# Three pairs of 1024 tokens instead of two, with the attention visits packed closer ahead of them

## The chip, the cores and the metric

The kernel runs on one core of a Trainium2 chip. The metric is the time on the device, in microseconds (us): the median of three runs of the kernel before is 894.93 us (894.25 to 895.53). A profiled execution of the same kernel took 893.7 us, of which 891.9 us lie between its first and its last instruction (the span).

## The reference, cut to what matters

Sliding-window attention (one half of the heads with a plain window of 32 keys, the other with 32 keys at a stride of 4) makes the tokens of a feed-forward layer:

```python
scores = scale * np.matmul(q, k.transpose(0, 1, 3, 2))      # q, k, v: 8 x 8 heads x 576 x 64
scores = np.where(masks[None], scores, -1e9)
attn = np.exp(scores - scores.max(-1)); attn /= attn.sum(-1) + 1e-9
x = np.matmul(attn, v).transpose(0, 2, 1, 3).reshape(4608, 512)
h = x @ w_in                                                # 512 -> 2048
sp = np.maximum(h, 0.0) + np.log1p(np.exp(-np.abs(h)))      # softplus
out = (h * erf(sp)) @ w_out                                 # 2048 -> 512
```

All is float32. The kernel keeps that accuracy by splitting each matmul operand into a high and a low part ("hi", "lo") and adding three products: hi*hi, hi*lo and lo*hi.

## The kernel before, in words

**Attention.** The work is cut into 72 units of 4 blocks of 64 queries. A visit (`attend`, `turn`, `mask_max`, `exponents`, `normalize`) takes one or two units and does, for units whose turn it is, transposes (L261) and values (L280), and for units three further on, scores (L222). VectorE (DVE) adds the mask and takes the maximum (L233), ScalarE (ACT) does the exponentials (L243) and copies finished rows out of PSUM (L322), GpSimd (POOL) multiplies by the inverse sums (L256). Masks of new units wait until ACT has copied the rows of the old ones out of the same PSUM banks. Finished rows go to HBM (`store_x`) and come back as the tokens of the feed-forward part.

**The feed-forward part** takes 9 chunks of 512 tokens. Per chunk there are 8 steps t (two blocks of 128 hidden features each), and each step has two half steps, numbered x = 2t and 2t+1. Three ways of doing the first product are in use:

- Chunks 0 to 2 (`mm1`, L526): 12 matmuls of 128x512 per half step into one PSUM bank `h`, which DVE copies out (`take`, L672).
- Chunks 3 and 4 (`mm1_fast`, L651): seven block products in place of eight (Winograd's form of Strassen's scheme) over the halves of one chunk, 42 matmuls of 128x256 per step; `take_fast` adds the products up.
- Chunks 5 to 8 as two pairs of 1024 tokens (`mm1_big`, L842): the same seven products with a whole chunk as each half, 42 matmuls of 128x512 per two blocks of features, so one such call serves two steps' worth of tokens. `take_big` adds them up (L850 to L862).

The block sums of the weights ("A11, S1 ...") are made once (`build`, x = 29 to 47) and kept in HBM (`ws`); `load_left` brings them back. The block sums of the tokens (B11, B21, B22, T1 to T4) are made by three kinds of job: `*_less` (DVE subtracts), `*_hi` (ACT writes the high part) and `*_lo` (DVE writes the low part).

**After h:** softplus and erf on ACT (L676, L679; L875, L952 in the pairs; each needs its table loaded), a product on DVE (L684, L879), the split into ghi and glo (L690, L691), and the second product on TensorE (PE), `mm2`, 12 matmuls of 128x512 per block of features into four PSUM banks (L715).

**Order.** All is one hand-written order; each engine works through its own instructions in that order and waits where a semaphore says so. First come 14 visits to single units, then 80 half steps x = 0 to 79 (chunks 0 to 4), then 34 *periods*. A period i does the second product of one item (24 matmuls): items 0 and 1 are the last two steps of the loop, then come A0 to A7 (first chunk of the pair), B0 to B7 (second chunk), A8 to A15, B8 to B15. Only the periods in `BIG` (0 to 7 and 16 to 23) also do a first product `mm1_big(d)`; the others (8 to 15, 24 to 33) have only the 24 matmuls. Items of kind B were put into HBM (`kept_g`) and come back by `load_g`; their ghi is cast by ACT, that of the other items by DVE. A period with a first product runs four groups of products with a quarter of the second product (6 matmuls) behind each:

```python
for u in pending: exponents(u)      # ACT: the units scored in the period before
split_item(item, 1)                 # ghi, glo of the item's second block
third(0); jobs(...); quarter()      # products 0, 1 and their take_big
third(1); ... Erf of A, B of d-1 ...; quarter()
... multiply_big("A", d-1); split_item(ahead, 0); third(2); turn(ready); quarter()
third(3); quarter(); attend(ready, scored); ... mask_max(scored)
```

`visits` says at which half steps (`PACE`) and in which periods (`late`) attention is visited. Before, two units are visited at 21 half steps from 17 to 65 and one unit at 9, 11 and 14; the last nine units are taken in periods 0 to 4. `FORE` and `AFT` say at which half step or period the jobs for a pair's token sums run.

## Time and profile before

| what | before |
|---|---|
| median of the runs | 894.93 us |
| profiled execution | 893.7 us, span 891.9 us |
| TensorE (PE) busy | 874.4 us, 98% |
| weight loads (PEld) | 718.1 us, 81% |
| VectorE (DVE) | 649.0 us, 73% |
| ScalarE (ACT) | 575.3 us, 65% |
| GpSimd (POOL) | 78.2 us, 9% |
| HBM traffic | 132.87 MB read, 41.94 MB written |

A row of a timeline is: start in us from the span's start, length in us, engine, line, operation, output<-inputs, shapes, count, and in brackets the idle time ahead of it with what ended it. Matmuls are pipelined, so the length of one matmul is longer than the distance to the next; what a stream of them costs is read from the starts. A row of the table by stretches is: stretch, its length, then the busy time and the count of instructions of each engine, the granted TensorE clock, the share of time that DMA engines are busy, and GB/s. A row of the groups is: line, engine, operation, names, shapes, count, then busy us and mean ns of one, then idle us before and what ended it.

### The profile page before, as it was taken

How to read it: one execution, taken by the hardware profiler on the slowest of the kernel's cores; microseconds unless marked ns; L12 is line 12 of the kernel's file. 1: busy time of each engine (PE TensorE's matmuls, PEld its weight loads, DVE VectorE, ACT ScalarE, POOL GpSimd, SP SyncE). 2: the span in 40 equal slices, each digit the busy share in tenths (PEclk: the TensorE clock that was granted, in tenths of full speed). 3: DMA queues.
4: the chain of work that ended last, by engine and by line, in shares of the span. 5: the costliest groups of instructions: out<-in, count | busy, mean ns of one | idle time of the engine just before them, and what ended most of it. 6: DMA issues, size and time to landing. Idle time of an engine off the chain costs nothing.

```text
span 891.9 us, 21528 instructions
## 1 busy us (share of the span) xinstructions
PE 874.4 (98%) x8470; PEld 718.1 (81%) x8470; DVE 649.0 (73%) x1623; ACT 575.3 (65%) x1265; POOL 78.2 (9%) x97
## 2 busy tenths in 40 slices
PE   7799999999999999999999999999999999999998
PEld 3367778888888888889889998888888888888886
DVE  5888878986789897767876886777566647575622
ACT  6889888886787786778877644764544434445321
POOL 2212110000111100111110000010000000000000
PEclk9999999999999999999999999999999999999999
DMA  8874444461678778589777753564449125442441
GB/s 284 293 252 150 125 143 133 149 205 55 226 256 299 277 255 295 194 318 311 243 246 262 261 184 137 194 238 170 166 161 358 48 82 208 158 156 81 149 134 49
DMA packets 67015, 176.24 MB, mean 198 GB/s; under 512 B 8288, under 2 KB 14688, under 8 KB 62816
## 3 DMA queue, kind: packets, MB, share of 16 engines
q1 hardware_dynamic: 66624, 174.32, 56.8%
q8 instruction: 67, 1.10, 0.5%
q10 hardware_dynamic: 288, 0.52, 0.2%
q14 instruction: 36, 0.29, 0.1%
HBM read 132.87 MB, written 41.94 MB: 196 GB/s over the span
## 4 chain that ended last, share of the span: by engine, by line
PE 92%; DVE 3%; ACT 2%; DMA 1%; issue 1%; POOL 0%; SPq 0%; POOLq 0%; DVEq 0%
PE acc L715 43%; PE h L526 14%; PE tx L842 9%; PE h L842 9%; PE h L651 5%; PE tx L651 4%; PE sp L280 3%; PE sp L222 3%; PE sp L261 1%; DMA dbl<-in_w_in_dram 1%; PE h L362 1%; ACT prob L243 1%; DVE s L684 0%; DVE w L463 0%; PE acc L280 0%
## 5 line engine op out<-in xcount | busy, mean ns | idle before, releaser
L715 PE MATMUL acc<-wout_hi,ghi 128*128 128x512 f32 x576 | 227.7, 395 | 0.2 <-DVE dbl L729 0.2
L715 PE MATMUL acc<-wout_lo,ghi 128*128 128x512 f32 x576 | 224.8, 390 | 0.0
L715 PE MATMUL acc<-wout_hi,glo 128*128 128x512 f32 x576 | 158.9, 389 | 0.0
L715 PEld LDWEIGHTS acc<-wout_hi,glo 128*128 128x128 f32 x576 | 108.1, 188 | 22.8
L715 PEld LDWEIGHTS acc<-wout_hi,ghi 128*128 128x128 f32 x576 | 108.3, 188 | 21.5 <-DVE dbl L729 0.6
L715 PEld LDWEIGHTS acc<-wout_lo,ghi 128*128 128x128 f32 x576 | 108.3, 188 | 21.0
L256 POOL TENSOR_TENSOR prob<-prob,rinv 128x256 f32<-128x256 f32 x72 | 70.7, 987 | 478.3 <-DVE rinv L255 230.0
L243 ACT ACTIVATE prob<-prob,nmax 128x64 f32<-128x64 f32 x288 | 96.4, 339 | 9.7 <-DVE nmax L233 9.3
L526 PE MATMUL h<-x,win 128*128 128x512 f32 x384 | 96.6, 394 | 0.6 <-DVE hc L672 0.6
L526 PEld LDWEIGHTS h<-x,win 128*128 128x128 f32 x384 | 71.2, 188 | 16.3 <-DVE hc L672 1.0
L233 DVE CUSTOM_DVE_ANT_0 prob<-sp,cst 128x64 f32<-128x64 f32 x288 | 45.2, 219 | 31.3 <-ACT rows L322 19.7
L676 ACT ACTIVATE s<-hc 128x1024 f32<-128x1024 f32 x40 | 42.5, 1062 | 37.1 <-DVE hc L665 22.5
L875 ACT ACT_TABLE_LOAD x16 | 20.5, 1283 | 70.8 <-DVE dbl L850 36.3
L322 ACT COPY rows<-sp 128x128 f32<-128x128 f32 (+7 forms) x167 | 27.8, 307 | 51.2 <-PE sp L222 51.1
L691 DVE TENSOR_TENSOR glo<-s,ghi 128x512 fp32r<-128x512 f32 x78 | 54.3, 696 | 2.7
L672 DVE COPY hc<-h 128x512 f32<-128x512 f32 x48 | 33.0, 688 | 30.1 <-PE h L526 29.8
L243 ACT ACTIVATION_READ_ACCUMULATOR prob<-prob,nmax 128x1 f32 x288 | 54.9, 191 | 0.0
L676 ACT ACT_TABLE_LOAD x40 | 51.3, 1283 | 0.7
L679 ACT ACT_TABLE_LOAD x40 | 51.3, 1283 | 0.7
L684 DVE TENSOR_TENSOR s<-hc,s 128x1024 f32<-128x1024 f32 x39 | 48.9, 1255 | 1.5 <-ACT s L679 1.5
L842 PE MATMUL h<-win 128*128 128x512 f32 x192 | 49.1, 391 | 0.0
L842 PE MATMUL tx<-win 128*128 128x512 f32 x192 | 49.1, 391 | 0.0
(176 smaller groups left out, 1518.2 us busy)
## 6 DMA issues: line engine op xcount, KB each, us to landing
win<-ws SPq DMA_DIRECT2D x32, 1024.0 KB, 5.4
win<-ws SPq DMA_DIRECT2D x32, 768.0 KB, 4.9
v<-in_v_dram SPq DMA_DIRECT2D x72, 256.0 KB, 4.4
qk<-in_qk_dram SPq DMA_DIRECT2D x48, 272.0 KB, 4.3
dbl<-in_w_in_dram SPq DMA_DIRECT2D x16, 512.0 KB, 4.3
dbl<-in_w_out_dram SPq DMA_DIRECT2D x16, 512.0 KB, 3.8
ws<-x SPq DMA_DIRECT2D x32, 256.0 KB, 2.9
qk<-in_qk_dram SPq DMA_DIRECT2D x24, 288.0 KB, 4.5
```

The lines of the kernel that those rows point to most:

```text
L233: nc.vector.tensor_tensor_reduce(out=pr[:, g, :], in0=sps[h][:, u % 2, p, :], in1=mask[QUADS.index(kinds(u, p))], scale=-SCALE, scalar=HUG ...
L243: nc.scalar.activation(out=probs[u][:, j, :], in_=probs[u][:, j, :], func=AF.Exp, scale=-1.0, bias=nmax[:, j:j + 1], accum_out=sums[u][:, ...
L256: nc.gpsimd.tensor_tensor(probs[u], probs[u], rinv.broadcast_to([P, 2 * PARTS, KEYS]), op=ALU.mult)
L526: nc.tensor.matmul(h, win_at[:, ftp, j, cc // 2, w, cc % 2, :], x[cc], start=(k == 0 and i == 0), stop=(k == CC - 1 and i == 2))
L651: nc.tensor.matmul((h, bank)[b][:, half * HN:(half + 1) * HN], w[:, k, wi, c, :], x[:, xi, c, :], start=(c == 0 and n == 0), stop=(c == 1 ...
L672: nc.vector.tensor_copy(out=hs[t][:, j], in_=h)
L676: nc.scalar.activation(out=ls[t], in_=hs[t], func=AF.Softplus)
L679: nc.scalar.activation(out=ls[t], in_=ls[t], func=AF.Erf)
L684: nc.vector.tensor_tensor(out=e, in0=hs[t], in1=ls[t], op=ALU.mult)
L691: nc.vector.tensor_tensor(out=glo, in0=e, in1=ghi.bitcast(F32), op=ALU.subtract)
L715: nc.tensor.matmul(args["out"], args["lhsT"], args["rhs"], start=args["start"], stop=args["stop"])
L842: nc.tensor.matmul(bank_, w[:, wi, c, :], x[c][:, xi, :], start=(c == 0 and n == 0), stop=(c == 1 and n == 2))
```

## The change

Chunks 3 and 4 leave the loop of half steps and become a first pair of 1024 tokens, so the loop ends after x = 47 (was 79), there are 50 periods, and `BIG` holds 0 to 7, 16 to 23 and 32 to 39. `mm1_fast`, `take_fast`, the jobs of `right` and their buffers go. Attention takes two units at 9, 13, 15 and at every odd half step from 17 to 39, none from 40 to 47, and the remaining units two at a time in periods 0 to 7 and 16 to 19. In `mm1` the first half step of a step writes bank `h` and the second writes bank `tx`; from t = 16 on the first one's copy is done by ACT (`late_take`). The token sums of the first pair are made at x = 41 to 47 and in period 0; those of the later pairs in periods 8 to 15 and 24 to 31.

```diff
-PAIRED = 5
+PAIRED = 3
+DOUBLES = (NCH - PAIRED) // 2
...
-PACE = [17, 21, 23, 27, 29, 31, 33, 35, 37, 39, 41, 47, 49, 51, 53, 55, 57, 59, 61, 63, 65]
-BIG = {**{d: d for d in range(SPC)}, **{d + SPC: d for d in range(SPC, 2 * SPC)}}
+PACE = [9, 13, 15] + list(range(17, 40, 2))
+BIG = {2 * SPC * k + d: SPC * k + d for k in range(DOUBLES) for d in range(SPC)}
...
-    while n < NU + LAG:
-        late[len(late)] = [i for i in (n, n + 1) if i < NU + LAG]
-        n += 2
+    for i in BIG:
+        if n < NU + LAG:
+            late[i] = [m for m in (n, n + 1) if m < NU + LAG]
+            n += 2
...
-                nc.tensor.matmul(h, win_at[:, ftp, j, cc // 2, w, cc % 2, :], x[cc],
+                nc.tensor.matmul((h, bank)[j], win_at[:, ftp, j, cc // 2, w, cc % 2, :], x[cc],
...
+    def late_take(t, j):
+        return j == 0 and t >= 2 * SPC
...
-        nc.vector.tensor_copy(out=hs[t][:, j], in_=h)
+        (nc.scalar.copy if late_take(t, j) else nc.vector.tensor_copy)(out=hs[t][:, j], in_=(h, bank)[j])
...
-    FORE = {68: [(big_load, 0)], 70: [LESS["T3"] + (room_w,)], 71: [LESS["T1"] + (room_w,), HI["B11"], HI["T3"]],
...
+    FORE = {41: [(big_load, 0, ("B22",), room_w), (big_load, 0, ("B12", "B11", "B21"))],
+            42: [LESS["T3"], HI["B11"]], 43: [LESS["T1"], HI["B21"]], 44: [LESS["T2"][:-1] + (room_of("B22"),)],
...
+            47: [LESS["T4"], LO["B21"], (big_places,), (big_load, 0, ("B22",)), HI["T3"], HI["T4"], HI["T1"]]}
+    AFT = {(0, 0): [LO["T3"]], (0, 1): [LO["T4"], HI["B22"]], (0, 2): [LO["T1"], LO["B22"]]}
...
-                (mm1_fast if fast else mm1)(t, j)
+                mm1(t, j)
...
-            right(x)
             jobs(FORE.get(x, ()))
```

Line numbers shift: in the changed kernel, L228 is the mask (was L233), L238 the exponentials (L243), L317 the rows (L322), L877 erf and L801 softplus in the pairs (L952, L875), L805 the product (L879), L611 and L612 ghi and glo (L690, L691), L778, L776 and L788 the sums of `take_big` (L852, L850, L862), L733 `big_lo` (L813), L605 the product of the loop (L684).

**ACT, where the last first product of a pair gives way to periods with the second product alone.** Before, the last erf of the first pair (L952, period 8) stands right behind the last softplus (L875, period 7), and the ghi of item B0 behind that:

```order
L952 ACT_TABLE_LOAD
L952 ACTIVATE s<-s 128x1024 x2
L875 ACT_TABLE_LOAD
L875 ACTIVATE s<-hc 128x1024 x2
L952 ACT_TABLE_LOAD
L952 ACTIVATE s<-s 128x1024 x2
L690 CAST ghi<-dbl_8443 128x512
```

Now, from the last softplus of d = 7 (period 7) to the ghi of item B0:

```order
L801 ACTIVATE s<-hc 128x1024 x2
L317 COPY rows<-sp_90 128x112
L317 COPY rows<-sp_90 128x16
L317 COPY rows<-sp_91 128x128
L317 COPY rows<-sp_90 128x128
L317 COPY rows<-sp_91 128x128
L238 ACT_TABLE_LOAD
L238 ACTIVATE prob,ssum<-prob,nmax 128x64 x8
L877 ACT_TABLE_LOAD
L877 ACTIVATE s<-s 128x1024 x2
L611 CAST ghi<-dbl_6596 128x512
```

The rows and eight exponentials with their table now stand between the last softplus and the last erf of the pair.

**DVE at period 17**, the second first-product period of a pair, whose item B7 gets its ghi from ACT (row L690 CAST ghi<-hc before, L611 now). Before, DVE's rows there are glo and then the sums of the new products:

```order
L850 TENSOR_TENSOR dbl_8791<-h,dbl_8791 128x512
L691 TENSOR_TENSOR glo<-hc,ghi 128x512
L852 COPY hc<-tx 128x512
L850 TENSOR_TENSOR hc<-h,hc 128x512
L850 TENSOR_TENSOR hc<-tx,hc 128x512
```

Now the masks of two units stand ahead of that glo (the last two of their sixteen rows shown), and on ACT the exponentials of these units stand ahead of the ghi it needs:

```order
L228 ISA prob,nmax<-sp_91,cst 128x64
L228 ISA nmax 128x1
L612 TENSOR_TENSOR glo<-hc,ghi 128x512
L778 COPY hc<-tx 128x512
L776 TENSOR_TENSOR hc<-h,hc 128x512
L776 TENSOR_TENSOR hc<-tx,hc 128x512
```

```order
L238 ACT_TABLE_LOAD
L238 ACTIVATE prob,ssum<-prob,nmax 128x64 x8
L611 CAST ghi<-hc 128x512
L877 ACT_TABLE_LOAD
L877 ACTIVATE s<-s 128x1024 x2
```

**DVE at period 0**, from the sums of products 0 and 1 to product 4. Before, one job stands among them (the low part of T1):

```order
L852 COPY dbl_7288<-h 128x512
L850 TENSOR_TENSOR dbl_7288<-tx,dbl_7288 128x512
L813 TENSOR_TENSOR x_97<-w,x_97 128x512
L813 TENSOR_TENSOR x_98<-w,x_98 128x512
L850 TENSOR_TENSOR dbl_7289<-h,dbl_7288 128x512
L850 TENSOR_TENSOR dbl_7289<-tx,dbl_7289 128x512
L684 TENSOR_TENSOR hc<-hc,s 128x1024
L690 CAST ghi<-hc 128x512
L691 TENSOR_TENSOR glo<-hc,ghi 128x512
L850 TENSOR_TENSOR dbl_7288<-h,dbl_7289 128x512
```

Now four jobs do (L733: T3, T4, T1, B22), and the low part of T1 (x_97, x_98), which product 5 reads, stands behind the product and the split of the next item:

```order
L733 TENSOR_TENSOR win<-w,win 128x512 x2
L776 TENSOR_TENSOR dbl_4978<-h,dbl_4977 128x512
L776 TENSOR_TENSOR dbl_4978<-tx,dbl_4978 128x512
L733 TENSOR_TENSOR x_99<-w,x_99 128x512
L733 TENSOR_TENSOR x_100<-w,x_100 128x512
L605 TENSOR_TENSOR hc<-hc,s 128x1024
L611 CAST ghi<-hc 128x512
L612 TENSOR_TENSOR glo<-hc,ghi 128x512
L733 TENSOR_TENSOR x_97<-pT_88,x_97 128x512
L733 TENSOR_TENSOR x_98<-o,x_98 128x512
```

The low part of T1 moved from between products 1 and 2 to behind the split of the next item, and three more jobs came in.

More of the change, by code (lines that the diff above doesn't have):

```diff
@@ L638, in right @@
-    def right(x):
-        c, at = divmod(x + READY, 2 * SPC)
-        if FAST <= c < PAIRED:
-            for job, *args in JOBS.get(at, ()):
-                job(c, *args)
-    def mm1_fast(t, j):
-        o, w = cells[STEPS[t][0]], left(t).rearrange("p (b i c n) -> p b i c n", b=len(LEFT), i=2, c=2)
-        for k in range(PART) if j == 0 else range(PART, len(LEFT)):
-            (b, half), x = PLACES[k], o[RIGHT[k]].rearrange("p i (c n) -> p i c n", c=2)
-            for c in range(2):
-                for n, (wi, xi) in enumerate(((0, 0), (0, 1), (1, 0))):
-                    nc.tensor.matmul((h, bank)[b][:, half * HN:(half + 1) * HN], w[:, k, wi, c, :], x[:, xi, c, :],
-                                     start=(c == 0 and n == 0), stop=(c == 1 and n == 2))
@@ L654, in take_fast @@
-    def take_fast(t, j):
-        if j == 0:
-            hs[t], ls[t] = (work.tile([P, PAIR, TOK], F32, name=n) for n in ("hc", "s"))
-        a = hs[t].rearrange("p f (k n) -> p (f k) n", k=2)
-        x, y = (q.rearrange("p (k n) -> p k n", k=2) for q in (h, bank))
-        if j == 0:
-            nc.vector.tensor_copy(out=a[:, 2], in_=y[:, 0])
-            nc.vector.tensor_tensor(out=a[:, 0:2], in0=x, in1=a[:, 2:3].broadcast_to([P, 2, HN]), op=ALU.add)
-            nc.vector.tensor_tensor(out=a[:, 2], in0=y[:, 1], in1=a[:, 1], op=ALU.add)
-        else:
-            nc.vector.tensor_tensor(out=a[:, 1::2], in0=y[:, 0:1].broadcast_to([P, 2, HN]), in1=a[:, 1:3], op=ALU.add)
-            nc.vector.tensor_tensor(out=a[:, 1:3], in0=x, in1=a[:, 1:3], op=ALU.add)
@@ L744, in store @@
             else:
-                if tt == 0 and c < FAST:
+                if tt == 0 and c < PAIRED - 1:
                     o = doubles(2).bitcast(F32).rearrange("p n w -> p (n w)")[:, 0:DM]
@@ L799, in room_p, with room_of @@
         return [pz[1], small.tile([P, DM], F32, name="o", bufs=1)]
-    def room_v():
-        return [v_.rearrange("p s h d -> p (s h d)") for v_ in vz]
-    def room_q():
-        return [q_[:, 0:TOK] for q_ in qkz]
+    def room_of(name):
+        return lambda: raw[name]
     def big_hi(name):
@@ L831, in jobs @@
             job(*args)
-    ITEMS = [NT - 2, NT - 1] + [(kind_, i * SPC + k) for i in range(2) for kind_ in "AB" for k in range(SPC)]
+    ITEMS = [NT - 2, NT - 1] + [(kind_, i * SPC + k) for i in range(DOUBLES) for kind_ in "AB" for k in range(SPC)]
     def mm1_big(d, k):
@@ L941, in period @@
         third(0)
-        if d is not None or i == SPC:
-            jobs(AFT.get(i, ()))
+        jobs(AFT.get((i, 0), ()))
         quarter()
@@ L966, in period @@
             split_item(ahead, 0)
+        jobs(AFT.get((i, 2), ()))
         last_ = 6 in groups[2]
@@ L984, in period @@
             load_g(ITEMS[i + 3])
-        if d is None and i != SPC:
-            jobs(AFT.get(i, ()))
+        jobs(AFT.get((i, 3), ()))
         for n in ns:
@@ L1048, in attn_moe_kernel @@
                 part_lo()
-                (take_fast if fast else take)(t, j)
-                if after is not None and j == PAIR - 1 and after < FAST:
+                if not late_take(t, j):
+                    take(t, j)
+                if after is not None and j == PAIR - 1:
                     load_x(after, range(twice, CC))
@@ L1057, in attn_moe_kernel @@
                 fresh, todo = todo, []
+            if late_take(t, j):
+                take(t, j)
             if j == 1 and 1 <= t <= NT:
```

118 lines of the change are left out of this document (37 added, 81 removed).

## The prediction

> **What bounds the kernel now.** I read the page's totals and the chain that ended last, then busy time by stretches, then the timelines of single stages.
>
> ```profile
> PE 874.4 (98%) x8470; PEld 718.1 (81%) x8470; DVE 649.0 (73%) x1623; ACT 575.3 (65%) x1265; POOL 78.2 (9%) x97
> ...
> PE 92%; DVE 3%; ACT 2%; DMA 1%; issue 1%; POOL 0%; SPq 0%; POOLq 0%; DVEq 0%
> ```
>
> ```profile
> core 0: us, PE busy (x) PEld busy (x) DVE busy (x) ACT busy (x) POOL busy (x), PEclk, DMA share, GB/s
> ...
> 49.00:94.70 45.70, 43.54 (x608) 33.59 (x607) 39.75 (x127) 41.53 (x113) 8.63 (x14) 1.00 0.62 205
> ...
> 173.00:200.00 27.00, 27.00 (x362) 22.11 (x362) 24.29 (x73) 24.08 (x66) 2.02 (x2) 1.00 0.58 195
> ...
> 246.00:306.00 60.00, 60.00 (x747) 49.22 (x748) 54.16 (x174) 48.87 (x140) 8.11 (x8) 1.00 0.79 279
> ...
> 713.50:830.50 117.00, 117.00 (x518) 96.85 (x517) 73.76 (x101) 51.33 (x48) 0.00 (x0) 1.00 0.37 131
> ```
>
> From 173 us on PE is never idle, though DVE and ACT are 90% busy at 173 to 200. So PE's own work sets the time: a microsecond of matmuls saved there is saved outright, and each microsecond in which PE waits for another engine is lost outright, with nothing behind it that could give it back.
>
> **1. Wider matmuls.** The first of these rows starts a step of chunk 4 without attention, the third starts the next step. The fourth starts period 16, the last starts period 17.
>
> ```profile
> 476.44 1.60 PE L651 MATMUL tx<-x,win 128*128 128x256 f32 x12
> 477.87 1.60 PE L651 MATMUL h<-x,win 128*128 128x256 f32 x12
> ...
> 486.96 1.24 PE L651 MATMUL tx<-x,win 128*128 128x256 f32 x9
> ...
> 713.54 1.52 PE L842 MATMUL h<-win 128*128 128x512 f32 x6
> 714.90 1.52 PE L842 MATMUL tx<-win 128*128 128x512 f32 x6
> ...
> 728.50 0.84 PE L842 MATMUL tx<-win 128*128 128x512 f32 x3
> ```
>
> Twelve matmuls of 256 columns take 477.87 - 476.44 = 1.43 us (119 ns each), six of 512 take 1.36 us (227 ns). A fast step is 10.52 us; period 16 (42 + 24 matmuls) is 14.96 us, and one with the second product alone is 24 x 0.227 = 5.44 us. Sixteen fast steps (168.3 us) become eight of each period (8 x 20.40 = 163.2 us): **-5.1 us**.
> [...]
>
> **2. Attention moves.** A fast step with two units lasts 374.78 - 361.78 = 13.00 us, so a visit there costs 2.48 us; a period with two lasts 17.70 us, 2.74 more than 14.96.
>
> ```profile
> 361.78 1.69 PE L651 MATMUL tx<-win 128*128 128x256 f32 x12
> ...
> 374.78 0.98 PE L651 MATMUL tx<-win 128*128 128x256 f32 x6
> ...
> 574.48 1.65 PE L842 MATMUL h<-win 128*128 128x512 f32 x6
> ...
> 592.18 1.20 PE L842 MATMUL tx<-win 128*128 128x512 f32 x4
> ```
>
> Nine visits leave fast steps, at most +0.26 us each; three single visits merge into pairs, which gives some of that back. Between 0 and +2.3 I take **+0.5**. With the visits go their four loads on SP and two multiplications on POOL; both have room there (131 GB/s moved in periods 16 to 23, the like of the new ones, against 279 in the steps with pairs; POOL is at 9%).
>
> **3. Two banks for h.** L526 waited 0.6 us for DVE's copies:
>
> ```profile
> L526 PE MATMUL h<-x,win 128*128 128x512 f32 x384 | 96.6, 394 | 0.6 <-DVE hc L672 0.6
> ```
>
> With the rest of such waits inside matmul lengths, bounds 0 and -1: **-0.5**. Early on DVE and ACT are behind it anyway.
>
> **4. Denser visits at x = 9 to 39.** The stretch 173 to 200 has two paired visits in a row with weight preparation, 246 to 306 has them with the weight sums; PE does not wait in either. **0**, because ACT and DVE have 10% left; without that cover, some 0.3 us in each of 7 steps (+2). ACT's copies of h from x = 32 on (8 of some 0.6 us) lie in its spare 11 of 60 us.
>
> **5. Token sums of the first pair.** DVE's prices, from starts: product 1.25, cast 0.46, glo 0.61, two `lo` or two `less` 1.21, copy 0.60.
>
> ```profile
> 335.16 1.21 DVE L684 TENSOR_TENSOR s<-hc,s 128x1024 f32<-128x1024 f32 x1
> 336.41 0.43 DVE L690 CAST ghi<-s 128x512 fp32r<-128x512 f32 x1
> 336.87 0.69 DVE L691 TENSOR_TENSOR glo<-s,ghi 128x512 fp32r<-128x512 f32 x1
> 337.48 1.28 DVE L625 TENSOR_TENSOR win<-w,win 128x512 fp32r<-128x512 f32 x2
> 338.69 0.68 DVE L672 COPY hc<-h 128x512 f32<-128x512 f32 x1
> 339.29 0.42 DVE L690 CAST ghi<-s 128x512 fp32r<-128x512 f32 x1
> ```
>
> At x = 41 to 46 there is no attention, and a step holds what this one, x = 43 and 44 before (sums of chunk 3 beside the weight sums), holds, less one copy on DVE:
>
> ```profile
> 318.80:329.70 10.90, 10.90 (x50) 9.00 (x49) 10.55 (x20) 10.82 (x18) 2.17 (x2) 1.00 0.73 273
> ```
>
> DVE is full there and PE does not idle, so it fits, barely. The ten loads of x = 41 stand on SP behind the writes of the weight sums of x = 40; DVE comes to the first of their data some 7 us later, and such loads took 5.6:
>
> ```profile
> win<-xT SPq DMA_DIRECT2D x2, 256.0 KB, 5.6
> ```
>
> Cover gone, 1 us. At x = 47 DVE starts when the last mm1 ends, 2.72 us before period 0: copy, product, split, T4, B21's lo = 0.60 + 1.25 + 1.07 + 1.21 + 1.21 = 5.34, so it is 2.6 us late; product 1's fifth matmul wants B21's lo at 2.27: 0.4 lost. Then DVE does split (3.7), two sums (4.9), T3's lo (6.1), the sum of product 2 (6.7), waits for product 3 (PE ends it at 7.3; sum 7.9), T4's lo (9.1), product (10.4), split (11.5), T1's lo (12.1, 12.7). PE: quarter to 4.6, products 2 and 3 to 7.3, quarter to 8.6, product 4 to 10.0; product 5 wants T1's lo at 10.2 and gets it at 12.1: 1.9 lost. **+2.3** (bounds +1 and +3.5).
>
> **6. Period 8.** The stage to read is the start of a period behind a paired visit, P = 592.18:
>
> ```profile
> 592.27 1.01 ACT L322 COPY rows<-sp 128x128 f32<-128x128 f32 x6 [0.62 <-PE sp L222]
> 593.39 1.28 ACT L243 ACT_TABLE_LOAD   x1
> ...
> 597.48 1.28 ACT L952 ACT_TABLE_LOAD   x1
> 598.77 2.01 ACT L952 ACTIVATE s<-s 128x1024 f32<-128x1024 f32 x2
> ```
>
> Rows, table and eight exponentials last until P + 5.3, erf of A until P + 7.6 (the two take 2.01). In period 8 the same chain stands ahead of A7, with only 5.44 us of second product to hide it. Without exponentials, before, erf ran at once and DVE's ghi of A7 came at 674.52 to 674.95:
>
> ```profile
> 673.20 1.23 DVE L879 TENSOR_TENSOR hc<-hc,s 128x1024 f32<-128x1024 f32 x1 [2.29 <-ACT s L952]
> 674.52 0.43 DVE L690 CAST ghi<-hc 128x512 fp32r<-128x512 f32 x1
> ```
>
> PE wanted it at 713.54 - 7 x 5.44 = 675.46, a margin of 0.5. Now: P + 7.6, product 1.25, cast 0.46 + 0.1 gives P + 9.4 against P + 5.6 (24 matmuls, and 0.15 for the first ones behind attention, as in the 4.24 of term 7 against 3 x 1.36): **+3.8** (bounds +3 and +4.5). Queued behind it on DVE are B7's product and A7's second split, needed 2.7 us later; no further wait.
>
> **7. Period 17.** Item B7's second ghi is ACT's, 0.62 us, behind the exponentials (P + 5.3). DVE's glo waits for it, and the sums of products 0 and 1 stand behind glo; product 2 needs the bank that the first sum frees.
>
> ```profile
> L690 ACT CAST ghi<-hc 128x512 fp32r<-128x512 f32 x16 | 10.0, 622 | 32.7 <-PE acc L715 32.7
> ```
>
> ```profile
> 577.97 0.69 DVE L852 COPY dbl<-h 128x512 f32<-128x512 f32 x1
> ...
> 578.72 1.66 PE L842 MATMUL h<-win 128*128 128x512 f32 x6
> ```
>
> With DVE's own cast (period 2, P = 574.48) that copy ends at 578.66 and product 2 starts at 578.72, P + 4.24, already at the edge. With ACT's: 5.3 + 0.62 + glo 0.61 + copy 0.69 = P + 7.2: **+3.0** (bounds +2 and +3.5).
>
> **8. The clock.** Only early does PE idle so long in this trace:
>
> ```profile
> 24.65 0.67 PE L280 MATMUL acc<-pT,v 64*64 64x32 f32 x32 [1.44 <-ACT pT L265]
> ```
>
> ```profile
> 8.17:11.59 3.42, 1.84 (x40) 1.00 0.94 311
> ...
> 21.83:25.24 3.41, 1.59 (x66) 1.00 0.93 327
> 25.24:28.65 3.41, 3.37 (x50) 0.50 0.78 281
> ```
>
> The last three rows are stretches of 3.41 us with PE's busy time, its instructions, the granted clock, DMA share and GB/s. After one with 1.59 us of PE work the granted clock was 0.50 for the next; after one with 1.84 it stayed 1.00. A wait of 3.8 us leaves some such stretch under 1.6 us of work whatever its phase, one of 3.0 us in most phases. Half clock for 3.41 us loses 1.7: **+3.4** for periods 8 and 17 (bounds 0 and +5.1, if period 0's wait does it too).
> [...]
>
> **Sum**, against the profiled 893.7 us: -5.1 + 0.5 - 0.5 + 2.3 + 3.8 + 3.0 + 3.4 = +7.4, so 901.1. The median of the runs is 1.2 us above the profiled execution, so **902.3 us**.
>
> **Rivals.**
> - *The clock falls at period 8 alone*, because 3.0 us leave each stretch more than 1.6 us of work: 902.3 - 1.7 = 900.6; *it falls nowhere*: 898.9. For: only one stretch in the trace shows the fall. Against: the numbers of term 8. Together 0.25. [...]
> - *ACT is not in the way* (faster): if masks and exponentials were done by P + 1.5, neither erf in period 8 nor ghi in period 17 waits, and no clock falls; only period 0 costs: -5.1 + 0.5 - 0.5 + 2.3 = -2.8, 892.1. It decides whether ghi of A7 comes by P + 5.6 and product 2's bank by P + 4.24. Against: the eight exponentials alone last 2.8 us, and the rows show them starting at P + 2.5. If period 0's wait is hidden too, -5.1, 889.8. Together 0.13.
> - *Smaller waits*: half of each and no clock loss, about 895 to 896: 0.10.
> - *DVE or DMA as a new bound at x = 13 to 47*: +2 by term 4 and 1 to 2 for late loads on top, 905 to 907: 0.10. For: 54.16 of 60.00 busy; against: no PE wait there.
>
> The forecast keeps 0.42. The range 895.5 to 905.5 leaves out the faster rival and part of the last one. A change under 0.2% (1.8 us) can't be told from none here: faster 0.13, same 0.08, slower 0.79.
>
> **What would show it.** PE's waits should be named in the trace: at the start of period 9 for DVE's ghi (L611), in period 17 for DVE's sum (L778), in period 0 for L733; the granted clock should read 0.5 for one stretch behind the first two; no other PE wait over 0.3 us beyond 130 us. If PE is not idle at period 9, I am wrong about what stands ahead of erf; if the total is under 893, the waits were covered.

## The result, and the profile after

The changed kernel takes 906.12 us (median of five runs, 905.62 to 907.53), the kernel before beside it 895.53 us (894.25 to 897.35): a ratio of 1.012, 95% interval 1.0104 to 1.0136, so 1.2% slower. The forecast was 902.3 us, with a range up to 905.5. The profiled execution took 906.74 us (span 904.9) against 893.7 (span 891.9): 13.0 us more, where the medians differ by 10.6. The last section comes back to that.

The totals of the page after, which answer to the first row shown of before:

```profile
PE 874.4 (97%) x8122; PEld 704.5 (78%) x8134; DVE 633.8 (70%) x1575; ACT 565.5 (62%) x1271; POOL 77.4 (9%) x97
```

PE is as busy as before with 348 matmuls fewer, because a matmul at half clock is busy for longer (10 fill 3.42 us in the rows of 0.50 below, 17 do at full clock in a row of e5_dummy further down), and this trace reads half clock for 17.1 us up to its last 20 us, that of before for 3.4; DVE and ACT are busy for less time than before. So no engine got more work, and the loss has to be in waits and in the clock. PE's waits in the trace after (line, what for; us in total, times, longest):

```profile
PE acc L636 <- DVE ghi L611: 3.7, 1, 3.7
PE tx L768 <- DVE hc L778: 3.6, 2, 2.6
...
PE tx L768 <- DVE x L733: 2.0, 1, 2.0
PE acc L636 <- DVE dbl L650: 2.0, 1, 2.0
...
PE tx L768 <- DVE win L733: 0.6, 1, 0.6
PE sp L275 <- DVE pT L260: 0.6, 1, 0.6
```

Five places. The first is period 8 to 9; the second holds period 17 (2.6) and period 7 (0.9); L733 is period 0; L650 is `save` at x = 11, which copies half-made sums out of the PSUM banks that `mm2` of x = 12 needs; the last row, for the transposed exponentials (pT), is the end of period 7 again.

The granted clock over stretches of 3.41 us, each pair a stretch with a wait and the one behind it (PE's busy time first, then the other engines', the clock, DMA share, GB/s), then the stretch that answers to 246 to 306 of before:

```profile
121.71:125.12 3.41, 1.44 (x7) 1.18 (x7) 3.38 (x6) 3.36 (x5) 0.00 (x0) 1.00 0.18 69
125.12:128.54 3.42, 3.42 (x10) 2.63 (x9) 0.77 (x2) 1.11 (x1) 0.00 (x0) 0.50 1.04 352
364.06:367.47 3.41, 1.67 (x7) 1.05 (x6) 3.20 (x5) 0.00 (x0) 0.00 (x0) 1.00 0.70 276
367.47:370.89 3.42, 3.15 (x16) 2.62 (x17) 3.31 (x6) 0.77 (x1) 0.00 (x0) 1.00 0.00 0
507.42:510.83 3.41, 0.49 (x2) 0.44 (x3) 2.09 (x3) 2.01 (x3) 0.00 (x0) 1.00 0.81 287
510.83:514.24 3.41, 3.41 (x10) 2.64 (x9) 2.42 (x4) 0.47 (x1) 0.00 (x0) 0.50 0.38 142
572.27:575.68 3.41, 1.05 (x5) 0.88 (x6) 1.98 (x3) 3.38 (x8) 0.00 (x0) 1.00 0.34 125
575.68:579.10 3.42, 3.42 (x10) 2.64 (x9) 0.69 (x1) 0.88 (x1) 0.00 (x0) 0.50 0.02 5
...
252.00:312.00 60.00, 60.00 (x870) 49.18 (x869) 52.55 (x157) 49.80 (x130) 9.51 (x9) 1.00 0.71 252
```

Behind the waits of the save, of period 8 and of period 17 the clock is 0.50 for one stretch (1.7 us lost each); behind period 0's it is not. In the last row, the densest visits with the weight sums, PE is busy for all 60 us, as it was before.

The wider matmuls gave what they should. The first products of periods 2 and 7 start at

```profile
393.07 1.66 PE L768 MATMUL h<-win 128*128 128x512 f32 x6
...
481.15 1.66 PE L768 MATMUL tx<-win 128*128 128x512 f32 x6
```

so five periods with two units take 88.08 us, 17.62 each; term 1 and term 2 used 17.70.

By stages, from the starts of PE's matmuls in both traces (up to the start of the last 252 matmuls, 830.50 us before and 844.03 after, 13.5 us apart):

| stage | length | without waits | excess | forecast |
|---|---|---|---|---|
| save, x = 11 to 13 | | | 2.0 + 1.7 | 0 |
| period 0 | 20.7 | 17.6 | 3.1 | 2.3 |
| period 7 | 19.8 | 17.6 | 2.2 | 0 |
| periods 8 to 15 | 49.3 | 8 x 5.44 = 43.5 | 5.7 | 3.8 + 1.7 |
| period 17 | 22.1 | 17.6 | 4.5 | 3.0 + 1.7 |
| what is left, by difference: terms 1 to 3 | | | -5.7 | -5.1 |

The forecast made +7.4 of this; the 6.1 us between are the save (3.7), period 7 (2.2), and 0.8 in period 0, less 0.6 in the rest.

Of the executions that the next section reads, one was disturbed, the profiled one of e1_ghi_first (1231 us at a mean clock of 0.654); its trace is not used.

### The profile page after: what moved, and what is told of

Same layout as the page of the kernel before. It is cut to its first block, busy times and chain, and to the rows that moved or that the text cites. A ratio compares the mean times of both kernels' runs of the same rounds, so it can differ in the third digit from the quotient of the medians.

```text
span 904.9 us, 20855 instructions
## 1 busy us (share of the span) xinstructions
PE 874.4 (97%) x8122; PEld 704.5 (78%) x8134; DVE 633.8 (70%) x1575; ACT 565.5 (62%) x1271; POOL 77.4 (9%) x97
## 5 line engine op out<-in xcount | busy, mean ns | idle before, releaser
L238 ACT ACTIVATE prob<-prob,nmax 128x64 f32<-128x64 f32 x288 | 96.4, 339 | 10.9 <-DVE nmax L228 10.7
L768 PE MATMUL tx<-win 128*128 128x512 f32 x288 | 74.9, 395 | 4.2 <-DVE hc L778 3.6
L228 DVE CUSTOM_DVE_ANT_0 prob<-sp,cst 128x64 f32<-128x64 f32 x288 | 45.3, 219 | 42.9 <-ACT rows L317 30.9
L768 PE MATMUL h<-win 128*128 128x512 f32 x288 | 75.2, 397 | 0.0
L768 PEld LDWEIGHTS tx<-win 128*128 128x128 f32 x288 | 53.5, 188 | 16.9 <-DVE hc L778 4.4
L768 PEld LDWEIGHTS h<-win 128*128 128x128 f32 x288 | 54.4, 191 | 12.3 <-DVE dbl L778 0.4
L612 DVE TENSOR_TENSOR glo<-hc,ghi 128x512 fp32r<-128x512 f32 x50 | 34.6, 692 | 38.3 <-PE acc L636 27.7
L238 ACT ACTIVATION_READ_ACCUMULATOR prob<-prob,nmax 128x1 f32 x288 | 54.9, 191 | 0.0
L612 DVE TENSOR_TENSOR glo<-dbl,ghi 128x512 fp32r<-128x512 f32 x48 | 33.2, 692 | 29.0 <-PE acc L636 17.5
L521 PE MATMUL h<-x,win 128*128 128x512 f32 x192 | 48.8, 396 | 0.0
L877 ACT ACTIVATE s<-s 128x1024 f32<-128x1024 f32 x48 | 48.2, 1052 | 0.3
L521 PE MATMUL tx<-x,win 128*128 128x512 f32 x192 | 48.0, 392 | 0.0
L801 ACT ACTIVATE s<-hc 128x1024 f32<-128x1024 f32 x24 | 25.5, 1061 | 35.4 <-DVE hc L776 22.9
L611 ACT CAST ghi<-hc 128x512 fp32r<-128x512 f32 x24 | 14.9, 622 | 49.1 <-PE acc L636 46.2
```

What stands on the lines that cost most here:

```text
L228: nc.vector.tensor_tensor_reduce(out=pr[:, g, :], in0=sps[h][:, u % 2, p, :], in1=mask[QUADS.index(kinds(u, p))], scale=-SCALE, scalar=HUG ...
L238: nc.scalar.activation(out=probs[u][:, j, :], in_=probs[u][:, j, :], func=AF.Exp, scale=-1.0, bias=nmax[:, j:j + 1], accum_out=sums[u][:, ...
L521: nc.tensor.matmul((h, bank)[j], win_at[:, ftp, j, cc // 2, w, cc % 2, :], x[cc], start=(k == 0 and i == 0), stop=(k == CC - 1 and i == 2))
L611: (copy or nc.vector.tensor_copy)(out=ghi, in_=e)
L612: nc.vector.tensor_tensor(out=glo, in0=e, in1=ghi.bitcast(F32), op=ALU.subtract)
L768: nc.tensor.matmul(bank_, w[:, wi, c, :], x[c][:, xi, :], start=(c == 0 and n == 0), stop=(c == 1 and n == 2))
```

## The experiments

Each kernel is the changed kernel with the edit shown. Its time is compared with the kernel before on the same chip (the changed kernel's ratio is 1.012). What an edit does to one stage is read from the trace, as the change in the distance to the changed kernel's trace over that stage: from x = 8 on two traces stay apart by a constant to within 0.1 us wherever no wait differs, while the times at which the traces reach x = 4 differ by up to 3.7 us. By the ratios alone e12, at the edge e13, and the five kernels with all edits are faster than the changed kernel, e4 is slower, and the others can't be told from it; what is said of those rests on their traces, one for each kernel.

| kernel | edit | median us | ratio to before (95%) |
|---|---|---|---|
| e1_ghi_first | period 17 | 904.06 | 1.0098 (1.0080 to 1.0116) |
| e2_erf_first | period 8 | 905.44 | 1.0120 (1.0094 to 1.0147) |
| e3_t1_early | period 0 | 905.44 | 1.0119 (1.0101 to 1.0136) |
| e4_visit11 | save | 908.94 | 1.0164 (1.0146 to 1.0183) |
| e11_save_first | save | 905.31 | 1.0119 (1.0098 to 1.0140) |
| e12_singles | save, periods 7, 8 | 901.60 | 1.0069 (1.0045 to 1.0092) |
| e13_ghi_groups | periods 17, 7 | 901.49 | 1.0079 (1.0054 to 1.0104) |
| e5_dummy | clock at period 9 | 905.45 | 1.0112 (1.0089 to 1.0135) |
| e6_one_bank | h in one bank | 908.38 | 1.0152 (1.0136 to 1.0168) |
| e15_fore46 | period 0 | 908.88 | 1.0151 (1.0129 to 1.0173) |
| e18_fore46_t1 | period 0 | 905.28 | 1.0118 (1.0101 to 1.0135) |
| e16_all | all | 895.58 | 1.0010 (0.9998 to 1.0023) |
| e20_all_t1 | all | 893.88 | 0.9995 (0.9986 to 1.0004) |
| e17_all7 | all, visit at x = 7 | 892.74 | 0.9984 (0.9968 to 0.9999) |
| e19_all7_t1 | the same | 892.38 | 0.9983 (0.9972 to 0.9995) |
| e21_all7_hole | the same | 891.49 | 0.9966 (0.9952 to 0.9979) |

### Period 17 and period 7: who stands ahead of ghi, and which product comes when

e1_ghi_first moves ACT's ghi ahead of the exponentials:

```diff
+        split_item(item, 1)
         for u in pending:
             exponents(u)
-        split_item(item, 1)
```

> In a period with a first product, ACT's ghi of the item's second half is issued ahead of the exponentials. Theory (a chain of its own for each wait): DVE's glo, and with it the sum that frees product 2's bank, no longer stands behind ACT's exponentials; PE's 2.6 us wait in period 17 goes and the half clock from 575.7 to 579.1 with it (1.7 us): 4.3 us faster than the changed kernel, some 901.8. Rival (the exponentials only start 0.6 us later and something else of the same period comes late): the wait stays above 1.5 us under another name, the time within 1 us of 906.1. Rival on the clock (its fall is not tied to that wait): 2.6 us faster and a half clock window near 576 still.

Its other three runs took 901.63 to 904.33 us. By the ratio to before that is 2.0 us better than the changed kernel, less than the 4.3 expected, and without a trace it decides nothing. So the edit was repeated, with one for period 7:

```diff
-            groups = [(0, 1, 2), (3, 4), (5, 6), ()]
+            groups = [(0, 1), (2, 3, 4), (5, 6), ()]
```

> Two edits in places that don't meet: in periods with a first product ACT's ghi of the item's second half ahead of the exponentials (period 17), and in periods 7 and 15 products 0, 1 in the first quarter and 2 to 4 in the second instead of 0 to 2 and 3, 4 (period 7). Theory: period 17 loses its 2.6 us wait, and the half clock if it fell there; period 7 loses 1.4 of the 2.2 us by which it is longer than a normal period with attention. Rival for 17: the wait keeps over 1.5 us under another name, because the exponentials then hold the masks' or take's next instruction. Rival for 7: product 2 waits for its bank in the second quarter as well, the period keeps its length, or A7's erf comes later and the wait at the start of period 9 grows by what was gained.

In the trace after, period 17: ACT casts ghi behind the exponentials, DVE's glo (L612) waits 3.66 us for it, the copy of product 0 (L778) stands behind glo, product 2 waits for the copy.

```profile
573.28 0.69 DVE L612 TENSOR_TENSOR glo<-hc,ghi 128x512 fp32r<-128x512 f32 x1 [3.66 <-ACT ghi L611]
573.89 0.68 DVE L778 COPY hc<-tx 128x512 f32<-128x512 f32 x1
...
574.62 2.05 PE L768 MATMUL tx<-win 128*128 128x512 f32 x6 [2.65 <-DVE hc L778]
```

With ghi ahead, the same period, in which product 2 starts with no wait at 4.24 us behind product 0:

```profile
564.43 1.66 PE L768 MATMUL tx<-win 128*128 128x512 f32 x6
...
568.67 1.52 PE L768 MATMUL tx<-win 128*128 128x512 f32 x6
```

Period 17 lost 4.6 us of its length: the wait and the half clock, the theory's 2.6 + 1.7. Period 7 lost 1.25 us. The cause there is the list of groups. The last period with first products has three of them ahead of the first quarter, so product 2 is wanted 2.7 us behind the start (at 483.9), while DVE still has a ghi and a glo ahead of the copy that frees its bank:

```profile
484.38 0.68 DVE L778 COPY hc<-tx 128x512 f32<-128x512 f32 x1
...
485.12 1.66 PE L768 MATMUL tx<-win 128*128 128x512 f32 x6 [0.93 <-DVE hc L778]
```

These groups were in the kernel before too. There the last such periods of its two pairs had no exponentials, no masks and no visit; now period 7 has all three. The rest of period 7's 2.2 us lies at its end, where the values wait for DVE's copy of pT; this wait is the same in e13 (0.59), and what makes DVE late there was not tested.

```profile
498.74 1.45 PE L275 MATMUL sp<-pT,v 64*64 64x32 f32 x64 [0.59 <-DVE pT L260]
```

### Period 8: erf behind the exponentials

```diff
+        erf_first = d is None
...
-        for u in pending:
-            exponents(u)
+        if not erf_first:
+            for u in pending:
+                exponents(u)
...
+        if erf_first:
+            for u in pending:
+                exponents(u)
         jobs(AFT.get((i, 1), ()))
         quarter()
-        while pending:
+        while pending and not erf_first:
             normalize(pending.pop(0))
...
             split_item(ahead, 0)
+        while pending:
+            normalize(pending.pop(0))
```

> In periods without a first product that have attention (7 to 8 and the last ones), the exponentials come behind the erf and the split of the next item, and the normalization behind that. Theory: A7's ghi comes in time, PE's 3.7 us wait at the start of period 9 goes and the half clock from 510.8 to 514.2 with it (1.7 us): 5.4 us faster, some 900.7. Rival (the exponentials are then late for the values): up to 2 us of it comes back as a wait of the values' matmuls for pT, 902 to 903. Rival on the clock: 3.7 us faster and the half clock still there.

The trace after shows the chain as forecast. Period 8 starts at 500.92; ACT's erf of A7 starts at 507.44, behind table and exponentials, and PE has done A6's 24 matmuls some 5.7 us after the start:

```profile
506.15 1.28 ACT L877 ACT_TABLE_LOAD   x1
507.44 2.00 ACT L877 ACTIVATE s<-s 128x1024 f32<-128x1024 f32 x2
...
508.53 1.23 DVE L805 TENSOR_TENSOR hc<-hc,s 128x1024 f32<-128x1024 f32 x1 [1.92 <-ACT s L877]
509.86 0.43 DVE L611 CAST ghi<-hc 128x512 fp32r<-128x512 f32 x1
...
510.34 0.50 PE L636 MATMUL acc<-wout_hi,ghi 128*128 128x512 f32 x1 [3.69 <-DVE ghi L611]
```

With erf first, periods 8 and 9 are 2.66 us shorter, the half clock is gone, and a wait of 2.33 us stands one half block later, for A7's second ghi:

```profile
511.82 0.17 DVE L249 TENSOR_SCALAR ssum<-ssum 128x4 f32<-128x4 f32 x1 [0.95 <-ACT prob L238]
512.10 0.18 DVE L250 RECIPROCAL rinv<-ssum 128x4 f32<-128x4 f32 x1
512.19 1.19 DVE L805 TENSOR_TENSOR hc<-hc,s 128x1024 f32<-128x1024 f32 x1
513.30 0.84 DVE L611 CAST ghi<-hc 128x512 fp32r<-128x512 f32 x1
```

DVE's product and ghi now stand behind its own `normalize`, which waits for the exponentials. The rival named the right kind of thing and the wrong place: not the values waited, but the next split. The ratio shows no gain (1.0120, as for the changed kernel); the 2.66 us are read from the trace. That A7's first ghi came in time once erf stood ahead shows that erf's late start was the cause of the first wait; taking the whole visit out (below) leaves 0.6 of the 3.7 us.

### The save at x = 11

The forecast gave this place nothing. First the visit of x = 9 was put there (`PACE = [11, 13, 15] + ...`):

> The single visit of x = 9 is put at x = 11 instead, in the step where the sums of the first weights are saved. Theory: with PE's attention in that step the copies of the save are hidden again, PE's 2.0 us wait in x = 12 and the half clock from 125.1 to 128.5 (1.7 us) go: 3 to 3.7 us faster, 902.4 to 903.1. Rival (DVE is as much later by the visit's own work as PE is): the wait stays above 1 us and the gain is under 1.5 us.

```profile
PE sp L275 <- ACT pT L650: 2.9, 1, 2.9
```

What moved is the pair of x = 9, not a single visit as the expectation calls it, and the edit was a bad one: the second unit's transposes lie in the tile that the save uses as its scratch, so that unit's values are taken from the saved sums, and PE now waits 2.9 us for the save's copy into it. Over x = 9 to 13, which hold the visit in both kernels, nothing was gained (0.6 us lost). It says nothing on the theory. A cleaner edit:

```diff
-                weights(x)
+                if x != SAVED:
+                    weights(x)
                 mm2(t - 2, j)
                 if x == SAVED:
                     save()
+                    weights(x)
```

> At x = 11 the preparation of weights comes behind the copies that save the sums, instead of ahead of them. Theory: PE's 2.0 us wait in x = 12 is the time that DVE's four instructions of that preparation (2.4 us) stand ahead of its two copies; it goes, and the half clock behind it with it where it fell: 2.0 to 3.7 us less by x = 14. Rival (the copies wait for PE's own last product, so that order on DVE is not the cause): the wait stays above 1.2 us. Rival (the weights come late instead): a wait for win or wout takes its place in x = 12 or 13.

DVE in the trace after, with PE's wait:

```profile
119.99 0.69 DVE L612 TENSOR_TENSOR glo<-s,ghi 128x512 fp32r<-128x512 f32 x1
120.60 0.68 DVE L453 TENSOR_TENSOR win<-w,win 128x512 fp32r<-128x512 f32 x1
...
122.99 0.68 DVE L650 COPY dbl<-acc 128x512 f32<-128x512 f32 x1
...
123.73 0.50 PE L636 MATMUL acc<-wout_hi,ghi 128*128 128x512 f32 x1 [1.97 <-DVE dbl L650]
```

and with the weights behind:

```profile
122.20 0.69 DVE L612 TENSOR_TENSOR glo<-s,ghi 128x512 fp32r<-128x512 f32 x1
122.81 0.68 DVE L650 COPY dbl<-acc 128x512 f32<-128x512 f32 x1
...
124.01 0.68 DVE L453 TENSOR_TENSOR win<-w,win 128x512 fp32r<-128x512 f32 x1
```

By x = 14 the kernel has gained 3.85 us (2.2 for the wait, 1.6 for the half clock: e3 and e13, which have the wait without the fall, are 1.6 us shorter than the changed kernel there), and no wait for weights came in its place. The kernel before has the order of the changed one and a single visit at x = 11:

```profile
122.13 0.68 DVE L729 COPY dbl<-acc 128x512 f32<-128x512 f32 x1
...
122.86 0.50 PE L715 MATMUL acc<-wout_hi,ghi 128*128 128x512 f32 x1 [0.16 <-DVE dbl L729]
```

Both kernels are best counted from the first matmul of x = 11 (112.92 before, 113.44 after). From there PE takes 9.78 us to this `mm2` in the kernel before and 8.32 us in the changed one, 1.46 less for want of the visit's transposes, values and scores. DVE's first copy starts 9.21 us behind that matmul before and 9.55 after: with the pair at x = 9, DVE has two units to normalize in place of one, and its product takes 1.61 us in place of 1.20, against one copy of pT less. Together that makes 2.0 us of waiting out of 0.2. DVE is as full in both kernels there; the row of the kernel before that answers to the one of 121.71 after:

```profile
121.71:125.12 3.41, 3.25 (x15) 2.36 (x14) 3.38 (x14) 1.46 (x9) 0.00 (x0) 1.00 0.44 169
```

The timed runs hardly show the gain (1.0119 against 1.0120), and the mean clock of both kernels' runs is the same, 0.99. Span times mean granted clock, an estimate of the time that a run would have had at full clock, is 894.4 us on average over this kernel's four runs and 896.1 over the changed kernel's five, but those five spread from 894.2 to 898.4: it fits the gain and does not prove it.

### Visits moved out of period 7

```diff
-    for x, n in zip(PACE, range(2 * NBLK + LAG, NU + LAG, 2)):
-        at[x] = [n, n + 1]
...
-    for i in BIG:
...
+    for x in sorted(PACE + [11, 14]):
+        k = 1 if x in (11, 14) else 2
+        at[x] = [n + m for m in range(k)]
+        n += k
+    for i in [i for i in BIG if i != SPC - 1]:
```

> Two single visits are put at x = 11 and 14, as the kernel before has them, and period 7's visit is left out for them; no work is added or removed. Theory: the exponentials in the way of A7's erf in period 8 are gone, and with them PE's 3.7 us wait and the half clock (5.4 us); period 7 loses the 2.2 us above a normal period with attention; the single visit at x = 11 hides most of the save's 2.0 us; the two visits cost on PE what period 7's cost: 8 to 11 us faster, 895 to 898. Rival (the exponentials were not the cause, product 3 to 7 of period 7 end too late for A7 anyway): the wait at the start of period 9 stays above 2 us and the gain is under 5 us. Rival (DVE is full at x = 9 to 15, and the two visits lose there what they gain later): over 3 us of new PE waits before x = 17.

Periods 7 to 9 became 8.4 us shorter, which includes the 2.7 us that period 7's visit itself takes; the wait for A7's ghi shrank from 3.7 to 0.6 us (the lines of this kernel are two higher: L638 is `mm2`, L652 the save, L613 the cast):

```profile
PE acc L638 <- DVE dbl L652: 0.8, 1, 0.8
...
PE acc L638 <- DVE ghi L613: 0.6, 1, 0.6
```

So period 7's visit was the cause in period 8, and by e2 it is its exponentials, which stood ahead of erf. The save's wait fell from 2.0 to 0.8, in what is one visit's work more on PE. At x = 14 a new wait of 1.16 us for the load of v came with the single visit; from the start of x = 11 to that of x = 16 the kernel is 1.6 us longer with the two visits, although the half clock there is gone. All told the kernel is 4.6 us faster than the changed one by its ratio and 7.5 by its trace from x = 4 on, of the 8 to 11 expected; 1.6 of the 7.5 is period 17's half clock, which did not fall in this trace.

### Period 0

Three orders of DVE's jobs. e3 puts T1's lo behind T4's (`(0, 1): [LO["T4"], LO["T1"], HI["B22"]]`) and B21's lo ahead of T4's sum at x = 47, e15 leaves T1 and moves both of the latter to x = 46, e18 does both with the jobs in their proper order:

```diff
-            45: [HI["T2"], LO["B11"]], 46: [LO["T2"]],
-            47: [LESS["T4"], LO["B21"], (big_places,), (big_load, 0, ("B22",)), HI["T3"], HI["T4"], HI["T1"]]}
+            45: [HI["T2"], LO["B11"]], 46: [LO["T2"], LESS["T4"], LO["B21"]],
+            47: [(big_places,), (big_load, 0, ("B22",)), HI["T3"], HI["T4"], HI["T1"]]}
```

> In period 0, T1's lo is made directly behind T4's, ahead of B22's two, and at x = 47 B21's lo stands ahead of T4's weight sum. Theory: both waits of product 1 and product 5 (0.9 and 2.4 us by the pitch of the matmuls) go: 3.3 us faster, some 902.8. Rival (DVE has too much to do in period 0 altogether, whatever the order): the wait moves to T4 or B22 and the gain is under 1 us.

In e3 T4's sum reads B21 where its lo has overwritten it, so the products with T4 are of other numbers; the work is the same.

> T4's weight sum and B21's lo (2.4 us on DVE) are issued in x = 46 behind T2's lo, instead of in x = 47 behind the last step's product and split. The trace of the changed kernel has DVE idle for 3.1 us there, waiting for the last matmuls of x = 47. Theory (period 0's waits are one chain of DVE, in order, that starts too late): everything behind comes 2.4 us earlier, product 1's 0.9 us and most of product 5's 2.4 us go, 2.7 to 3.3 us gained in period 0. Rival (what the reordering of T1's lo showed, DVE has too much to do inside period 0 itself): product 1's wait alone goes and the gain is under 1.2 us.

> T4's sum and B21's lo at x = 46 as before this, and T1's lo directly behind T4's lo too, ahead of the product and split of the next item. Theory: with the first edit alone product 1's wait went (0.9 us) and DVE had 3 us of holes in period 0, in which it waited for PE's products; product 5's 2.0 to 2.4 us come from the place of T1's lo in DVE's order alone, and now go: period 0 is 3.0 us or more shorter than in the changed kernel. Rival (DVE's amount of work): the wait moves to the banks' sums (L776) and the gain beyond the 0.9 us stays under 0.8 us, as when T1's lo was moved without the first edit.

PE's waits in period 0: after (by product: 1, 5), e18 (6).

```profile
357.17 1.44 PE L768 MATMUL tx<-win 128*128 128x512 f32 x5 [0.60 <-DVE win L733]
...
367.74 1.43 PE L768 MATMUL tx<-x,win 128*128 128x512 f32 x5 [2.01 <-DVE x L733]
```

```profile
369.91 0.94 PE L768 MATMUL h<-dbl,win 128*128 128x512 f32 x3 [1.54 <-DVE dbl L776]
```

Gained in period 0: e3 0.6 us, e15 0.9 us (product 1's wait alone), e18 1.4 us; in e3 and e18 the wait at product 5 goes and one at product 6 comes, for the sum that frees its bank. Up to here the rival (too much work) was ahead. The trace of e18 has DVE idle for 0.8 us early in the period, between two sums, and busy without a hole from 363.0 to 369.1. e21 therefore puts T1's lo one place earlier, into that hole (`(0, 0): [LO["T3"], LO["T1"]]`), in the kernel with all other edits:

> As the kernel with all edits, the visit at x = 7 and T1's lo behind T4's, but with T1's lo one place earlier still, behind T3's. In the trace DVE is idle there for 0.8 us between two of its sums and then busy without a hole for 6 us, at the end of which PE waits 1.5 us for a sum. Theory (the order within period 0 decides): 1.2 us of work moves out of the full stretch into the hole, the wait at product 6 shrinks by 0.8 to 1.2 us, some 891.3. Rival (what is moved delays the sums of products 2 and 3, and those PE's next products): no gain, a wait for h or tx of 0.4 us or more earlier in period 0.

```profile
PE h L768 <- DVE dbl L776: 0.3, 1, 0.3
```

The wait fell from 1.5 to 0.3 us, and period 0 gained 2.6 of its 3.1 us over the changed kernel, without an instruction less on DVE (2.4 us of its work now lie in x = 46). So the order of its work, and not the amount, held PE there, and it took three moves because each only handed the wait on to the next job in DVE's line.

### The clock by itself

```diff
         split_item(item, 1)
+        if i == SPC + 1:
+            for _ in range(15):
+                nc.tensor.matmul(h, wout_hi[:, 0, 0:P], wout_hi[:, 1, :], start=True, stop=True)
         third(0)
```

> Fifteen matmuls of 128x512 whose result nobody reads (3.4 us at 227 ns) stand on PE at the start of period 9, ahead of A7's products, where PE is idle for 3.7 us. They add PE work and take nothing away. Theory (the clock is cut because a stretch of 3.41 us holds too little matmul work): the half clock behind period 9's start is gone, the 24 matmuls behind it run at 227 ns, 1.7 us gained though work was added; period 8 to 9 shortens by 1.5 to 1.7 us. Rival (the half clock has another cause, or the dummies delay A7): no gain, up to 0.4 us lost, and the granted clock reads 0.5 there still.

The stretches at the same place:

```profile
508.86:512.27 3.41, 3.11 (x14) 2.30 (x13) 2.08 (x3) 2.03 (x3) 0.00 (x0) 1.00 0.82 283
512.27:515.69 3.42, 3.42 (x17) 2.79 (x16) 3.20 (x6) 0.62 (x1) 0.00 (x0) 1.00 0.38 140
```

The clock stays at 1.00 and the stage is 1.6 us shorter with 15 matmuls more in it. So the half clock came of the matmul work missing from that stretch (0.49 us of it in the trace after, 3.11 here): A7's ghi was no earlier.

### One bank for h

`mm1` writes to `h` again, `take` copies from it, and `late_take` returns False.

> h of single chunks goes to one bank again and its copies all to DVE, as before; nothing else is undone. Theory: the second bank brought nothing, since the early steps wait for other things and the later ones for nothing; 0.5 us slower at most, within what the early steps vary from run to run. Rival (the two banks carry the dense visits at x = 9 to 39): PE's waits for hc L593 come back, 0.3 us or more in several of those steps, 2 us and more slower by x = 47.

```profile
PE h L521 <- DVE hc L593: 0.9, 2, 0.7
```

0.4 us slower in the steps x = 8 and 9, and within 0.1 us from x = 10 to 47. The rest of its longer time, like that of e15, lies in the steps before x = 4 (1.3 and 3.2 us more than the changed kernel in their traces). The traces read half clock there for 13.7 us in e15 and for 6.8 in both e6 and the changed kernel, so the clock can account for e15 and not for e6; what else varies stays open. The second bank, with ACT's copies, is worth the half microsecond of term 3 and does not carry the dense visits.

### All edits together

e16 joins e12, e13, e15 and e11; e20 adds T1's lo of e18; e17 and e19 are the same with period 7's visit as a pair at x = 7 (`PACE = [7, 9, 13, 15] + ...`) in place of the two singles, e21 as above.

> Single visits at x = 11 and 14 in place of period 7's, the save ahead of the weights at x = 11, ghi ahead of the exponentials, the order of products in periods 7 and 15, T4's sum and B21's lo at x = 46. Theory (each wait is a chain of its own, prices add): 8.0 for the visits, 4.5 for ghi, 2.7 to 3.3 for period 0, 0.8 for what is left of the save, 1.2 for period 7, that is 17 us less than the changed kernel: some 889, 0.6% faster than the kernel before. Rival (the waits share a bound, DVE or ACT, that now comes up elsewhere): less than 12 us, 894 or more, no faster than before.

> The kernel with all edits and single visits at x = 11 and 14, with T1's lo moved too. Theory: 2.4 to 4.1 us less than the same kernel without it: some 892. Against the pair at x = 7 it tells whether two single visits are dearer than a pair at a free place: up to 2.6 us slower than that kernel by theory, the same by the rival (a visit costs the same everywhere).

> As the kernel with all edits, but period 7's visit goes to x = 7 as a pair, and x = 11 and 14 have none. Theory: the 2.7 us that the two single visits cost at x = 12 to 15 are not paid, and x = 7 has room, as PE ran there without a wait: 886 to 888. Rival: at x = 7 the visit's loads or the exponentials of the first units are not there yet, and 2 us or more are lost before x = 9.

> The kernel with all edits and period 7's visit at x = 7, with T1's lo moved too. Theory: 2.0 to 2.4 us less in period 0, and the half clock behind it (1.7 us) gone, so 2.4 to 4.1 us less than the same kernel without it: some 889 to 890. Rival: within 1 us of it.

From x = 4 to the last 252 matmuls e16 gained 12.8 us on the changed kernel, e20 13.4, e17 11.0, e19 14.6 and e21 15.9 in their traces. The prices nearly add: for e21 3.85 (save), 2.6 (period 0), 8.4 (periods 7 to 9), 4.6 (period 17) less 3.5 for the visit at x = 7 (3.3 in e19, 4.4 in e17), 15.9 in all, of which the 2.6 and the 3.5 are e21's own. In e21 periods 7 to 9 gained 9.4 and periods 11 and 12 lost 1.0 again, part of it a wait for ACT's ghi.

e16 and e17 stayed dearer since period 0's wait, 2.0 us alone now, took the clock down in both. By the medians four of the five fell short of their theories: e16 895.58 us against 889 (its rival said 894 or more), e17 892.74 against 886 to 888, e20 893.88 against 892, and e19 892.38 against 889 to 890, within 1 us of e17 as its rival said. e21 came out as forecast (891.49 against 891.3). The pair at x = 7 costs 0.6 to 1.7 us more than the 2.7 of a pair in a period, in part for a load of v (a wait of 1.07 us in e17), as its rival had it, and is still the cheaper place by the medians (892.38 against 893.88 us). e21 is 0.34% faster than the kernel before (0.9966, 0.9952 to 0.9979).

## Why the prediction was wrong

The sign and four of the eight terms (1, 6, 7 and, in this trace, 8) were right; the size was short by 6.1 us in the trace, and the median lies 0.6 us above the range. The missing 6.1 us are almost all in two places that the sum put at nothing, the save (3.7) and period 7 (2.2).

- **Term 1** (wider matmuls, -5.1) held: the new periods run at 17.62 us against 17.70.
- **Terms 2 and 3** (+0.5, -0.5): with term 1 they came to -5.7 by difference, which leaves no room for dearer visits where PE has no wait; e6 puts the second bank at 0.4.
- **Term 4** ("0, because ACT and DVE have 10% left") is the step that failed. It read the cover from shares of DVE's time over the stretches 173 to 200 and 246 to 306, and asked only about steps that get a visit. The step that lost its visit, x = 11, was not asked about. There DVE is 99% busy in both kernels (3.38 of 3.41 us), so its share could not tell; the save's copies are late in both, and the visit was the PE work that lay beside them. Without it PE waits 2.0 us, and the clock took 1.6 more. e11 shows that the wait is for the copies' place in DVE's order, e12 that a single visit put back takes it down to 0.8; the rest is, by DVE's rows, the pair at x = 9, which no usable run took away.
- **Term 5** (period 0, +2.3): the two waits and their places held, product 1's 0.4 was 0.9, product 5's 1.9 was 2.4 by the starts of the matmuls. The kernel with all edits and T1's lo in the hole (e21) shows that DVE's order makes them.
- **Term 6** (+3.8): 3.7. ghi came at 9.4 us behind the start, as worked out. **Term 7** (+3.0): 2.65.
- **Term 8** (+3.4) held in this trace for the two places it named and left out a third, the save. e5 shows its mechanism. At period 17 that was luck: the clock fell behind this wait in five traces of ten (last section), where the term had "in most phases".
- **Period 7** was in no term. Term 7's reasoning, that the take of product 0 must be done before product 2 wants its bank, applies to a period with three products in its first group even when DVE casts ghi itself. The groups were not read for the one period that is a last one and has a visit: 2.2 us, 1.25 of them shown by e13. The sign that the prediction set itself, no other PE wait over 0.3 us beyond 130 us, failed here (0.93 and 0.59 us); its border at 130 us left the save's wait out.

The rival "DVE or DMA as a new bound at x = 13 to 47" gave the right total (905 to 907) by luck, for a reason that is not there: PE has no wait from x = 17 to 47. "ACT is not in the way" and "smaller waits" are refuted by the wait rows.

## What to carry to other kernels

When a change takes a piece of work away from a step, look at what that piece covered there, instruction by instruction, before asking what the piece costs at its new place; a busy share over a longer stretch says nothing on one step. When work moves into a period with its own variant of the order (a last one, a first one), walk that variant. In an order kept strictly on each engine a wait is seldom removed by one move: read the next job in line, and move until the trace has work in the hole.
